# Second MoE: the transposes of an item's third and fourth tile put into branches on the item's count

## The chip, the cores and the metric

One core of one Trainium2 chip runs the kernel. The metric is the device time of one execution in microseconds (us), as the median of several runs. The profile is of one further execution of the same program on the chip.

## The reference, cut to what matters

Three layers follow one another: windowed attention, a gated feed-forward layer (called the first MoE here, though it has one expert), and a mixture of eight experts (the second MoE), which is the part that the change touches:

```python
x = _moe_ref(x=x, **moe_kwargs)                 # 2304 rows of 512
logits = x @ w_gate                             # 8 experts
expert_idx = np.argmax(logits, axis=1)
...
for e in range(8):
    mask = expert_idx == e
    xe = x[mask]
    h = np.maximum(xe @ w1[e], 0.0)             # 512 -> 1024
    ye = h @ w2[e]                              # 1024 -> 512
    out[mask] = gate_w[mask, None] * ye
```

How many rows an expert gets depends on the data and is known only while the kernel runs.

## The kernel before

The second MoE works through nine **items**. An item is a number of tiles of 128 rows of one expert: items 0 and 1 are the first and the second pair of tiles of expert 0, items 2 to 8 are four tiles each of experts 1 to 7. (Rows beyond 512 of one expert are done in a loop behind it, `L1200`, that is skipped when there are none.) Each item has eight steps f = 0 to 7, one for each 128 of the 1024 hidden columns. In a step TensorE does `first_mm` (rows by w1, 12 matmuls: four pieces of the depth by three products, since every float32 operand is split into a high and a low part), and `out_c` for the step before (hidden by w2, three matmuls of 512 columns for each tile of rows). ScalarE and VectorE make the ReLU and its two parts (`relu`), and split the weights of two steps ahead (`c_split`).

The order on each engine is as written out by hand in the loop over `steps2`; the compiler reorders nothing. All engines run their own list in order and wait for each other by semaphores.

**The count.** Only the rows that an expert has are worth computing. `load_count` (L1007) reads the count of an item's expert from SBUF into a register of TensorE. `cases` (L1029) then makes a tree of branches on TensorE alone, with one arm for each multiple of 64 rows from 256 to 512: `first_mm` runs over that many columns and `out_c` over that many tiles. For items 2 to 8 an arm is reached by two or three comparisons, in item 1 by one. The first two tiles are always done.

**The transposes.** The rows of the next item lie in SBUF with a row on each partition, and `first_mm` needs them transposed. `c_transpose(i, j, bk)` does tile j of item i: four TensorE transposes (L890) into one PSUM bank, ScalarE's copy of it (L892, the high part) and VectorE's subtraction (L893, the low part). Tiles 0 to 3 of item i + 1 are transposed at the ends of the steps f = 2, 3, 4 and 5 of item i, into banks 2 and 3 in turn. All four are done whatever the count.

So at the end of step f = 4 of item i, TensorE's list is: the arm of `cases`, `out_c` of tiles 0 and 1 (six matmuls, the last of them `bank<-who,hl`), the four transposes of tile 2, and then the comparisons of `cases` of step 5. In step f = 5 `load_count(i + 1)` stands ahead of the transposes of tile 3.

Of the kernel before, what the change touches and what calls it, by code (L numbers as in the profile page):

```python
# [26 lines left out]
P = 128  # L27
# [26 lines left out]
def attention_moe_moe_kernel(ctx, tc, qT, kT, vw, w1p, rms_g, wg2, wg2T, w2p, out):  # L54
    nc = tc.nc
# [14 lines left out]
    ident = const.tile([P, P], F32, name="ident")  # L70
# [53 lines left out]
    def xt_views(at, n):  # L124

        return [xt_t[:, a:a + 4 * n].rearrange("p (c t) -> p c t", c=4) for a in (at, at + 4 * n)]
# [160 lines left out]
    def beside(tasks, budget, fresh=True):  # L287

        for t in tasks if fresh else []:
            t.rest = 0.0  # L290
        while budget > 0:
            can = [t for t in tasks if not t.done and t.rest <= 0 and t.want != "bank"
                   and not (callable(t.want) and not t.want())]
            if not can:
                break
            cost = can[0].piece()
            budget -= cost
            for o in tasks:
                if o is not can[0]:
                    o.rest -= cost  # L300
        return budget

    def on_bank(tasks, bk):

        for t in tasks:
            if t.want == "bank" and not t.done:
                return t.piece(bk)
        return 0.0
# [395 lines left out]
    def out_b(u):  # L704
        k, i = units[u]
        last_mm(k, ("b", u), enumerate(out_banks(i)), u == starts[i], u == stops[i])
# [3 lines left out]
    def evac(u):  # L710
        k, i = units[u]
        n = steps[k][0]
        if u != stops[i]:
            return 0.0
        t0, nt, _ = subs[i]
        for j, bk in enumerate(out_banks(i)):
            x2 = x2_p.tile([P, DM], F32, name="x2")
            (nc.vector.tensor_copy if j % 2 else nc.scalar.copy)(x2, bk)
            x2_t.setdefault(n, []).append(x2)
            nc.sync.dma_start(x2dram[t0 + j * P:t0 + (j + 1) * P], x2)  # L720
        if i == blocks[n][2][-1]:
            put[0] = n
        return 0.6
# [119 lines left out]
    items = [(0, 0, 2), (0, 2, 2)] + [(e, 0, 4) for e in range(1, E)]  # L843
    steps2 = [(i, f) for i in range(len(items)) for f in range(NF2)]
    K0 = len(steps)
    ix_t, xg_t = {}, {}
# [11 lines left out]
    def c_split(k, hold=False, parts="ao"):  # L858
        if k < len(steps2):
            rest = w_split(K0 + k, ("c", k), wring[w_index(k) % NRING], 512, {"a": nc.vector, "o": nc.vector},  # L860
                           parts)
            if not hold:
                for _, r in rest:
                    r()
            if k >= NF2 and "o" in parts:
                later.append(w_index(k) + NRING)
            return rest
# [15 lines left out]
    def c_transpose(i, j, bk):  # L883
        if i >= len(items) or j >= items[i][2]:
            return
        if j == 0:
            xh_t["c", i], xl_t["c", i] = xt_views(i % 2 * 8 * 512, 512)
        xh, xl, ts = xh_t["c", i], xl_t["c", i], slice(j * P, (j + 1) * P)
        for c in range(4):
            nc.tensor.transpose(bk[:, c * P:(c + 1) * P], xg_t[i][:, j, c * P:(c + 1) * P], ident)  # L890
        b3 = bk.rearrange("p (c t) -> p c t", c=4)
        nc.scalar.copy(xh[:, :, ts], b3)  # L892
        nc.vector.tensor_tensor(out=xl[:, :, ts], in0=b3, in1=xh[:, :, ts].bitcast(F32), op=ALU.subtract)  # L893
# [38 lines left out]
    for u, (k, i) in enumerate(units):  # L932
# [7 lines left out]
        if len(blocks[n][2]) > 1:  # L940
            bk = bank[1]
        else:
            bk = bank[4] if n == len(blocks) - 1 else bank[5]
# [58 lines left out]
    count = {}  # L1002
# [18 lines left out]
    def cases(i, body, unit=P // 2):  # L1021

        e, t0, T = items[i]

        def between(lo, hi):
            if lo == hi:
                return body(lo * unit)
            mid = (lo + hi) // 2
            with tc.If(count[e] > t0 * P + mid * unit) as more:  # L1029
                between(mid + 1, hi)  # L1030
            with more.Else():
                between(lo, mid)

        if i == 0:
            body(T * P)
        elif T == 4:
            between(2 * P // unit, T * P // unit)
        else:
            unit = P
            between(1, T)  # L1040

    def first_mm(k, n):
        i, f = steps2[k]
        wh, wl = wh_t[K0 + k, "a"], wl_t[K0 + k, "a"]
        xh, xl, n = xh_t["c", i], xl_t["c", i], max(n, 2 * P)
        for c in range(4):
            w = slice(c * P, (c + 1) * P)
            split_mm(bank[k % 2][:, :n], wh[:, w], wl[:, w], xh[:, c, :n], xl[:, c, :n], c == 0, c == 3)

    def relu(k):  # L1050
        n = items[steps2[k][0]][2] * P
        if k == NL - 1:
            hh, hl = (xt_t[:, a:a + 512] for a in (16 * 512, 17 * 512))
        else:
            hh, hl = (h_p.tile([P, 512], F32R, name=x) for x in ("hh", "hl"))
        hh_t[K0 + k], hl_t[K0 + k] = hh, hl
        nc.scalar.activation(hh[:, :n], bank[k % 2][:, :n], AF.Relu, scale=1.0)  # L1057
        nc.vector.scalar_tensor_tensor(out=hl[:, :n], in0=bank[k % 2][:, :n], scalar=0.0, in1=hh[:, :n].bitcast(F32),  # L1058
                                       op0=ALU.max, op1=ALU.subtract)

    def out_c(k, n, j0=0):
        f = steps2[k][1]
        last_mm(K0 + k, K0 + k, [(j, bank[4 + j]) for j in range(j0, -(-n // P))], f == 0, f == NF2 - 1)
# [14 lines left out]
    def c_out(i, tiles=None):  # L1078
        ix = ix_t[i]
        for j in tiles or range(items[i][2]):  # L1080
            y = x2_p.tile([P, DM], F32, name="x2")
            gw = ix[:, j, 1:2].bitcast(F32)
            if j % 2:
                nc.vector.tensor_scalar_mul(y, bank[4 + j], gw)
            else:
                nc.scalar.activation(y, bank[4 + j], AF.Copy, scale=gw)  # L1086
            d = nc.gpsimd.indirect_dma_start(out=out[:, :], in_=y, in_offset=None,  # L1087
                                             out_offset=bass.IndirectOffsetOnAxis(ap=ix[:, j, 0:1], axis=0),
                                             bounds_check=NT - 1, oob_is_err=False)
            tc.declare_no_dep(d.ins, group="out", reason="a token has one expert: the rows differ")  # L1090
            tc.add_to_no_dep_group("out", d.ins)
# [44 lines left out]
    for k, (i, f) in enumerate(steps2):  # L1136
        if i == 0:
            for now in range(2):
                if now == (k > 1):
                    first_mm(k, 2 * P)  # L1140
                elif k > 0:
                    on_bank([end], bank[3])
                    beside([end], 99)
            if k == 0:
                out_b(len(units) - 1)
            else:
                out_c(k - 1, 2 * P)
        elif i == 1:
            if f < 2:
                if f == 0:  # L1150
                    out_c(k - 1, 2 * P)
                first_mm(k, 2 * P)
                if f == 1:
                    cases(i, lambda n: out_c(k - 1, n))
            else:
                cases(i, lambda n: (first_mm(k, n), out_c(k - 1, n)))
        elif f > 0:
            cases(i, lambda n: (first_mm(k, n), out_c(k - 1, n, 2)))
            if k < NL - 1:
                out_c(k - 1, 2 * P)  # L1160
        else:
            j0 = 0 if i == 2 else 1
            cases(i, lambda n: first_mm(k, n))
            out_c(k - 1, j0 * P)
            cases(i - 1, lambda n: out_c(k - 1, n, j0), P)
        relu(k)
        if k == 0:
            evac(len(units) - 1)
        if f == 0 and i > 0:
            c_split(k + 2, parts="a")  # L1170
            c_out(i - 1)
            c_split(k + 2, parts="o")
        else:
            c_split(k + 2)
        while i > 0 and later:
            c_load(later.pop(0))
        if i == 0:
            if f == NF2 - 1:
                end.finish(bank[3])
                load_count(1)  # L1180
                for j in range(2):
                    c_transpose(1, j, bank[2 + j % 2])
            continue
        if f == 5:
            load_count(i + 1)
        beside([over], 0.4)
        if i == len(items) - 1 and f == 3:

            nc.gpsimd.drain()
        if f in (2, 3, 4, 5):  # L1190
            c_transpose(i + 1, f - 2, bank[2 + f % 2])
        if f == 6:
            c_gather(i + 2)
# [6 lines left out]
    with tc.If(n_over > 0):  # L1200
        with tc.For_i(0, n_over, 1) as i:
            ex = nc.values_load(slot[0:1, bass.ds(i, 1)], engines=(ET.SP,), min_val=0, max_val=E - 1)
            row = nc.values_load(slot[0:1, bass.ds(i + NS, 1)], engines=(ET.SP,), min_val=0, max_val=E * NT - 2 * P)
            with tc.tile_pool(name="ovr", bufs=1) as o_p:
# [14 lines left out]
                for f in range(NF2):  # L1219
                    bk = bank[2 + f % 2][:, :2 * P]  # L1220
# [58 lines left out]
```

## Time and profile before

| | us |
|---|---|
| median of 3 runs | 831.22 (829.57 to 832.62) |
| the profiled execution, its own time | 828.35 |
| its span in the trace | 826.6 |

The span is what the trace covers, from the first to the last instruction; the profiled execution's time is 1.75 us longer, for what lies around it. In the views, PE is TensorE's matmuls, PEld its weight loads, DVE is VectorE, ACT ScalarE, POOL GpSimd, SP SyncE. A letter q behind an engine marks its sequencer: waits, branches, register work. A row such as `bank<-xt,wha` says what an instruction writes and reads. L60 is the helper that issues every matmul. Matmuls are pipelined, and the end of each is modelled by the profiler, so the time from one start to the next is the better measure of what one costs.

### The profile page before, as it was taken

To read this page: it belongs to the slowest core of one execution; us is meant where nothing else is said; L and a number is where in the kernel's file an instruction comes from. 1 tells how busy PE (TensorE), PEld (TensorE's weight loads), DVE (VectorE), ACT (ScalarE), POOL (GpSimd) and SP (SyncE) were. 2 spreads that over 40 slices of the span, in tenths; PEclk is the share of its full clock that TensorE was granted. 3 is DMA by queue.
4 is the path that set the end of the run, shared out by engine and by line. 5 is a ranking of instruction groups with operands and counts; after the bars stand their busy time and mean duration, and the time that the engine had idled before them with its cause. 6 is when DMAs were issued, how large, how long until landed. Compare 5 with 4: busy or idle time off the path is not lost. (4 is left out here: it accounts for less than half of the span.)

```text
span 826.6 us, 13258 instructions
## 1 busy us (share of the span) xinstructions
PE 806.6 (98%) x4777; PEld 746.5 (90%) x4777; DVE 566.7 (69%) x1210; ACT 431.1 (52%) x839; POOL 222.1 (27%) x194
## 2 busy tenths in 40 slices
PE   7999999999999999999999999999899999999997
PEld 7999989899999999999899999999788999888886
DVE  6898777777754766763389869846595765776454
ACT  5878877677633323322343333434564654765353
POOL 7989444334340000015000006031300220222021
PEclk9999999999999999999999999999999999999999
DMA  8999679889422101002110023861675763772010
GB/s 273 327 294 303 154 183 249 224 174 273 128 103 77 38 1 39 1 1 76 40 38 1 1 81 112 266 170 62 159 252 193 232 231 113 260 252 81 2 45 22
DMA packets 76179, 114.33 MB, mean 138 GB/s; under 512 B 28847, under 2 KB 45615, under 8 KB 75954
## 3 DMA queue, kind: packets, MB, share of 16 engines
q1 hardware_dynamic: 71506, 103.50, 42.5%
q0 software_dynamic: 4576, 9.47, 3.1%
q8 instruction: 69, 1.13, 0.6%
q14 instruction: 28, 0.23, 0.1%
HBM read 93.90 MB, written 31.10 MB: 151 GB/s over the span
## 5 line engine op out<-in xcount | busy, mean ns | idle before, releaser
L60 PE MATMUL bank<-xt,wha 128*128 128x384 f32 (+3 forms) x1728 | 417.9, 327 | 1.9 <-ACT xt L892 1.3
L60 PEld LDWEIGHTS bank<-xt,wha 128*128 128x128 f32 x1728 | 301.8, 188 | 10.9 <-ACT xt L892 1.5
L60 PE MATMUL bank<-xt,wla 128*128 128x384 f32 (+3 forms) x864 | 280.0, 324 | 0.3 <-DVE wla L576 0.3
L60 PEld LDWEIGHTS bank<-xt,wla 128*128 128x128 f32 x864 | 162.7, 188 | 1.0 <-DVE wla L576 0.6
L60 PE MATMUL bank<-who,hl 128*128 128x512 f32 x382 | 150.2, 393 | 1.0 <-DVE hl L1058 0.6
L60 PE MATMUL bank<-who,hh 128*128 128x512 f32 x382 | 150.3, 393 | 0.2 <-ACT x L1086 0.2
L60 PE MATMUL bank<-wlo,hh 128*128 128x512 f32 x382 | 149.4, 391 | 0.0
L685 ACT CAST hh<-t 128x384 fp32r<-128x384 f32 x72 | 37.0, 514 | 149.4 <-DVE t L684 149.4
L576 DVE TENSOR_TENSOR wla<-wraw,wha 128x512 fp32r<-128x512 f32 (+1 forms) x113 | 99.2, 878 | 15.9 <-ACT wha L574 15.2
L1058 DVE SCALAR_TENSOR_TENSOR hl<-bank,hh 128x512 fp32r<-128x512 f32 (+1 forms) x71 | 44.7, 629 | 70.9 <-ACT hh L1057 70.8
L684 DVE TENSOR_TENSOR t<-t,bank 128x384 f32<-128x384 f32 x72 | 39.7, 552 | 74.1 <-PE bank L60 67.9
L574 ACT CAST wha<-wraw 128x512 fp32r<-128x512 f32 (+1 forms) x113 | 87.0, 770 | 6.0 <-DVE wraw L426 5.8
L1087 POOL DMA_INDIRECT out_dram<-x,ix x32 | 34.8, 1086 | 204.1 <-ACT x L1086 196.6
L60 PEld LDWEIGHTS bank<-who,hl 128*128 128x128 f32 x382 | 71.8, 188 | 18.2 <-DVE hl L1058 1.4
L1057 ACT ACTIVATE hh<-bank 128x512 fp32r<-128x512 f32 (+1 forms) x71 | 39.0, 550 | 89.3 <-PE bank L60 89.3
L60 PEld LDWEIGHTS bank<-who,hh 128*128 128x128 f32 x382 | 72.0, 189 | 10.4 <-ACT x L1086 0.4
L60 PEld LDWEIGHTS bank<-wlo,hh 128*128 128x128 f32 x382 | 72.0, 189 | 10.2
L574 ACT CAST who<-wraw 128x512 fp32r<-128x512 f32 x111 | 68.7, 619 | 17.5 <-PE bank L60 17.5
L749 DVE SCALAR_TENSOR_TENSOR junk<-x,wg_bc 128x512 f32<-128x512 f32 x120 | 76.6, 685 | 0.0
L576 DVE TENSOR_TENSOR wlo<-wraw,who 128x512 fp32r<-128x512 f32 x99 | 68.2, 689 | 8.6 <-ACT who L574 3.4
L683 ACT ACTIVATE t<-bank 128x384 f32<-128x384 f32 x72 | 35.0, 486 | 65.7 <-PE bank L60 62.7
L797 POOL TENSOR_TENSOR tot<-tot,ohb 128x8 f32<-128x8 f32 x18 | 4.5, 251 | 237.6 <-DVE de L781 236.5
(154 smaller groups left out, 969.9 us busy)
## 6 DMA issues: line engine op xcount, KB each, us to landing
wraw<-in_w2p_dram SPq DMA_DIRECT2D x64, 512.0 KB, 4.6
st<-in_w1p_dram SPq DMA_DIRECT2D x24, 768.0 KB, 7.3
wraw<-in_vw_dram SPq DMA_DIRECT2D x16, 512.0 KB, 5.9
xs<-x2dram SPq DMA_DIRECT2D x8, 1024.0 KB, 12.8
qs<-in_qT_dram SPq DMA_DIRECT2D x16, 288.0 KB, 5.9
xdram<-wraw SPq DMA_DIRECT2D x32, 144.0 KB, 4.6
x2dram<-x SPq DMA_DIRECT2D x18, 256.0 KB, 2.0
kt<-in_kT_dram SPq DMA_DIRECT2D x15, 288.0 KB, 5.4
```

The source lines that it names most:

```text
L60: nc.tensor.matmul(o, l, r, start=start, stop=stop)
L574: nc.scalar.copy(wh, src[:, r])
L576: e.tensor_tensor(out=wl, in0=src[:, r], in1=wh.bitcast(F32), op=ALU.subtract)))
L683: nc.scalar.activation(t, g, AF.Silu, scale=1.0)
L684: nc.vector.tensor_tensor(out=t, in0=t, in1=v, op=ALU.mult)
L685: nc.scalar.copy(hh[:, :nt], t)
L749: nc.vector.scalar_tensor_tensor(out=junk, in0=x2, scalar=1.0, in1=wg_bc[:, e], op0=ALU.mult, op1=ALU.mult, accum_out=lg[:, j, e:e + 1])
L797: nc.gpsimd.tensor_tensor(out=tot, in0=tot, in1=ohb[:, j], op=ALU.add)
L1057: nc.scalar.activation(hh[:, :n], bank[k % 2][:, :n], AF.Relu, scale=1.0)
L1058: nc.vector.scalar_tensor_tensor(out=hl[:, :n], in0=bank[k % 2][:, :n], scalar=0.0, in1=hh[:, :n].bitcast(F32), op0=ALU.max, op1=ALU.subtract)
L1087: d = nc.gpsimd.indirect_dma_start(out=out[:, :], in_=y, in_offset=None, out_offset=bass.IndirectOffsetOnAxis(ap=ix[:, j, 0:1], axis=0), b ...
```

## The change

For the third and fourth tile of an item (j = 2 and 3) the four transposes stand in a branch of TensorE that is taken only if the count of the item's expert reaches into that tile. ScalarE's copy and VectorE's subtraction stay outside and run in any case. Since the count is now needed by step f = 4, it is loaded in step f = 2 and no longer in step f = 5. Items 2 to 8 have a third and a fourth tile, so there are 14 such branches.

```diff
@@ -886,8 +886,16 @@
         if j == 0:
             xh_t["c", i], xl_t["c", i] = xt_views(i % 2 * 8 * 512, 512)
         xh, xl, ts = xh_t["c", i], xl_t["c", i], slice(j * P, (j + 1) * P)
-        for c in range(4):
-            nc.tensor.transpose(bk[:, c * P:(c + 1) * P], xg_t[i][:, j, c * P:(c + 1) * P], ident)
+
+        def turn():
+            for c in range(4):
+                nc.tensor.transpose(bk[:, c * P:(c + 1) * P], xg_t[i][:, j, c * P:(c + 1) * P], ident)
+
+        if j < 2:
+            turn()
+        else:
+            with tc.If(count[items[i][0]] > j * P):
+                turn()
         b3 = bk.rearrange("p (c t) -> p c t", c=4)
         nc.scalar.copy(xh[:, :, ts], b3)
         nc.vector.tensor_tensor(out=xl[:, :, ts], in0=b3, in1=xh[:, :, ts].bitcast(F32), op=ALU.subtract)
@@ -1181,7 +1189,7 @@
                 for j in range(2):
                     c_transpose(1, j, bank[2 + j % 2])
             continue
-        if f == 5:
+        if f == 2:
             load_count(i + 1)
         beside([over], 0.4)
         if i == len(items) - 1 and f == 3:
```

## Rows read from the trace of the kernel before

**Rows 1.** The page, busy time: engine, busy us, share of the span, instructions.

```profile
PE 806.6 (98%) x4777; PEld 746.5 (90%) x4777; DVE 566.7 (69%) x1210; ACT 431.1 (52%) x839; POOL 222.1 (27%) x194
```

**Rows 2.** Busy time by stretch of the second MoE, with clock and DMA share.

```profile
core 0: us, PE busy (x) PEld busy (x) DVE busy (x) ACT busy (x) POOL busy (x), PEclk, DMA share, GB/s
585.00:600.00 15.00, 12.07 (x78) 10.06 (x77) 7.96 (x16) 7.39 (x15) 2.47 (x4) 1.00 0.68 196
...
655.00:700.00 45.00, 45.00 (x259) 40.91 (x258) 29.02 (x45) 25.16 (x45) 4.82 (x4) 1.00 0.54 180
...
735.00:745.00 10.00, 8.72 (x57) 7.55 (x57) 6.55 (x11) 5.62 (x11) 2.38 (x2) 1.00 0.90 312
745.00:815.00 70.00, 70.00 (x388) 62.30 (x387) 40.72 (x63) 35.02 (x62) 8.74 (x8) 1.00 0.10 36
```

**Rows 3.** Groups by form on PE: first_mm of items 2 to 8, in order.

```profile
L60 PE MATMUL bank<-xt,wha 128*128 128x320 f32 x64 | 14.7, 315 | 0.2 <-ACT wha L574 0.2
...
L60 PE MATMUL bank<-xt,wha 128*128 128x256 f32 x63 | 11.8, 284 | 0.0
...
L60 PE MATMUL bank<-xt,wha 128*128 128x384 f32 x56 | 14.6, 341 | 0.0
...
L60 PE MATMUL bank<-xt,wha 128*128 128x256 f32 x64 | 12.1, 286 | 0.0
...
L60 PE MATMUL bank<-xt,wha 128*128 128x256 f32 x64 | 12.0, 285 | 1.3 <-ACT xt L892 1.3
...
L60 PE MATMUL bank<-xt,wha 128*128 128x448 f32 x61 | 17.6, 368 | 0.0
...
L60 PE MATMUL bank<-xt,wha 128*128 128x256 f32 x54 | 9.9, 280 | 0.0
```

**Rows 4.** PE's timeline (start us, us), a step's end with and without transposes.

```profile
715.51 0.39 PE L60 MATMUL bank<-who,hl 128*128 128x512 f32 x1
715.75 0.60 PE L890 MATMUL bank<-ident,xr 128*128 128x128 f32 x4
716.10 0.48 PE L60 MATMUL bank<-xt,wha 128*128 128x256 f32 x2
716.42 0.28 PE L60 MATMUL bank<-xt,wla 128*128 128x256 f32 x1
...
666.38 0.40 PE L60 MATMUL bank<-xt,wha 128*128 128x256 f32 x2
666.63 0.28 PE L60 MATMUL bank<-xt,wla 128*128 128x256 f32 x1
```

**Rows 5.** L1029's branches, a step's three, and PE's timeline where that step begins.

```profile
L1029 PEldq COMPARE_BRANCH  x3: 208/208/208, 742.4 to 742.9; - x3
...
745.07 0.48 PE L60 MATMUL bank<-xt,wha 128*128 128x256 f32 x2
```

**Rows 6.** L1200, a skipped branch (min/median/max ns, first and last start); PE's last matmul.

```profile
L1200 PEldq COMPARE_BRANCH  x1: 342/342/342, 818.6 to 818.6; - x1
...
L1200 PEldq EVENT_SEMAPHORE  x1: 51/51/51, 820.9 to 820.9; - x1
...
820.49 0.40 PE L60 MATMUL bank<-who,hl 128*128 128x512 f32 x1
```

**Rows 7.** L1029's branches at the start of item 2, and PE's timeline there.

```profile
L1029 PEldq COMPARE_BRANCH  x3: 70/208/208, 612.3 to 612.8; - x3
...
612.27 0.49 PE L60 MATMUL bank<-who,hl 128*128 128x512 f32 x1
612.93 0.55 PE L60 MATMUL bank<-xt,wha 128*128 128x320 f32 x2 [0.16 <-ACT wha L574]
```

**Rows 8.** L1029's branches in all, and those of two steps of item 5.

```profile
L1029 PEldq COMPARE_BRANCH  x200: 70/208/3600, 593.6 to 814.9; - x100
...
L1029 PEldq COMPARE_BRANCH  x3: 208/208/697, 713.4 to 714.5; - x3
...
L1029 PEldq COMPARE_BRANCH  x3: 208/208/637, 716.7 to 717.6; - x3
```

**Rows 9.** L1029's longest branch, and PE's timeline behind it.

```profile
L1029 PEldq COMPARE_BRANCH  x3: 208/208/3600, 737.6 to 741.5; - x3
...
739.93 0.60 PE L890 MATMUL bank<-ident,sq 128*128 128x128 f32 x4
741.81 0.50 PE L60 MATMUL bank<-xt,wha 128*128 128x256 f32 x2 [1.28 <-ACT xt L892]
```

**Rows 10.** L1007's loading of a count in item 1, and PE's timeline there.

```profile
L1007 PEldq TENSOR_LOAD <-cnt x1: 329/329/329, 607.0 to 607.0; - x1
...
607.25 0.40 PE L60 MATMUL bank<-who,hl 128*128 128x512 f32 x1
607.67 0.65 PE L890 MATMUL bank<-ident,xr 128*128 128x128 f32 x4
```

## The prediction

> **What bounds the kernel now.** I read the page first: TensorE is busy 806.6 of 826.6 us, VectorE 69%, ScalarE 52% [rows 1]. Then the stretches of the second MoE: PE fills 45.00 of 45.00 us and 70.00 of 70.00, and what it misses lies at the start and in 735 to 745 [rows 2]. So a microsecond that TensorE saves or loses here moves the end by the same. [...]
>
> Next, what is skipped. The widths of first_mm tell each item's count within 64: 320, 256, 384, 256, 256, 448, 256 for items 2 to 8 [rows 3]. The third tile is needed above 256, so in items 2, 4 and 7; the fourth above 384, in item 7 alone. Of 14 branches four run their transposes and ten skip them.
>
> What remains is the branch itself. PE's timeline shows no branch, so I asked for the branches by their source line. Three comparisons start at 742.4 to 742.9, but the step that they choose begins on PE at 745.07 [rows 5]: TensorE's sequencer runs about 2.4 us ahead of its matmuls, and under that lead the branches of today cost nothing. The question is whether the new ones leave the lead alone.
>
> **What the change removes.** From the last who,hl matmul of a step to the next first_mm is 0.59 us (715.51 to 716.10), 0.35 of it the four transposes (715.75 to 716.10). Behind transposes the first pair of matmuls also goes slower: 716.10 to 716.42 against 666.38 to 666.63, 0.07 us [rows 4]. Ten skips would give 10 x (0.35 + 0.07) = 4.2 us, if nothing took their place.
>
> **What it adds in a skip.** The last transpose raises TensorE's semaphore, by which ScalarE's copy knows that the bank is filled. A path around it must raise it too. The kernel has one branch without an else that is skipped already, L1200: TensorE's comparison ends at 818.6 + 0.34 = 818.9, and then an EVENT_SEMAPHORE of that same line comes, but only at 820.9, when PE's last matmul, begun at 820.49, has ended at 820.89 [rows 6]. So a skipped branch makes up for the missed increment in the sequencer, and waits for every matmul issued before. The arms of L1029 escape that because each holds matmuls; an empty arm does not. I therefore expect each of the ten skips to **drain TensorE**, and with it the 2.4 us of lead goes.
>
> Queued behind that wait is all of TensorE: next in its list are the comparisons of the next step's cases, then the first weight load. They now pass in the open. With S the start of the last who,hl: the semaphore instruction comes at S + 0.41 to 0.45 (820.49 to 820.9, read to a tenth), takes 0.05 [rows 6], and a hand-over in the sequencer takes some 0.06, so the sequencer is free at S + 0.55.
>
> The price of open comparisons is shown at the start of item 2, where the lead is gone: comparisons of 208, 208 and 70 ns run from 612.3, and first_mm starts at 612.93, although the matmul ahead had started at 612.27 [rows 7]. That is 0.66 us for two of 208 and one of 70 ns, which fits 0.27 for each of the first kind and 0.13 for the second, hand-overs included. (The row blames ACT for the gap; the comparisons explain it.) I read 208 ns as a comparison that goes to its else arm, as all three do at width 256 [rows 5], and 70 ns as one that falls into its then arm.
>
> By widths [rows 3], a skip in an item costs, start of first_mm after against S + 0.59 before:
> - items 3 and 5 (width 256, three of 208): S + 0.55 + 0.81 = S + 1.36, so 0.77 us, three times: 2.31;
> - item 2 (320): S + 0.55 + 0.67 = S + 1.22, 0.63 us, twice: 1.26;
> - items 4 and 7 (384 and 448, one of 208 and one of 70): S + 0.95, 0.36 us, four times: 1.44;
> - item 1 (one of 208): S + 0.82, 0.23 us, once.
>
> Sum 5.24 us. The skips counted are those of the next item's tiles, done in the steps of the item named. The 0.07 us of a slow start stays, since first_mm behind an open branch starts slowly too (612.93). The skip's own comparison lies under the matmuls still queued, so nothing is added for it.
>
> [...]
>
> **Late comparisons.** Some take longer than 208 ns: 637 and 697 in the sets ahead of the two steps of item 5 that would follow a skip, up to 3600 in all [rows 8]. Today the lead hides them, save one: the 3600 ns one began at 737.9 and held PE from 739.93 + 0.35 to 741.81, about 1.5 us [rows 9]. In the open all of the excess counts. Added over the ten sets that would be exposed, it is 1.7 us in this execution, of which item 5's two sets are 0.49 + 0.43 [rows 8]. Bounds: nothing, if the wait gives time to have the instructions at hand, and 10 x 0.49 = 4.9 if every set were as late as the worst of item 5. I take 1.7, since it is the same code at the same places.
>
> **What it moves.** The loading of the count goes from f = 5 to f = 2, the same instructions, no DMA. In items 2 to 7 the lead hides it at both places. In item 1 there is little lead: it begins at 607.0 and the transposes start at 607.67, 0.42 us behind the matmul ahead where 0.24 is usual [rows 4, 10]. That 0.18 goes, and about 0.3 comes at f = 2, where PE waits for VectorE and the lead is just as small: 0.1 net, between 0 and 0.4.
>
> **What stays.** The four branches that run: a 70 ns comparison and a jump over the else path, under the lead: 0 us, up to 4 x 0.3 = 1.2 if it is short. ScalarE's copy and VectorE's subtraction run as before; PE waits on neither in the full stretches [rows 2]. GpSimd, SP and the DMA queues get nothing new.
>
> **Sum:** 5.2 + 1.7 + 0.1 = 7.0 us slower. The profiled execution of 828.35 would become 835.4. It stood 2.9 us below the median of 831.22, so against that median I forecast 838.2.
>
> **Rivals.**
> - *The skip does not drain* (faster). If the increment is made up without waiting for earlier matmuls, the lead survives and PE goes from who,hl to first_mm in 0.23 us, as where no transposes stand. Then all 4.2 us come back, less 0.1: 827.1. For it: PE is full and removed work counts whole [rows 2]. Against it: the two idle microseconds of L1200's semaphore [rows 6]. It decides if the semaphore instruction of a skip runs while PE still has matmuls queued. 0.13.
> - *The drain is cheap* (within 0.3%, that is 2.5 us, about what a measurement of this kernel can tell from no change). PE's ends are modelled; if the semaphore rises nearer to the next usual start, S + 0.23, each skip is 0.2 us cheaper, and with no late comparisons the sum falls to 5.2 - 2.0 = 3.2; with the one 1.5 us hold-up [rows 9] gone as well, 1.7 remain: 832.9. 0.07.
> - *Code comes late in the open* (slower still). Every comparison after a drain that has to wait as at 737.9 now costs 3.4 us over its 208 ns instead of 1.5 [rows 9]. If three of ten sets met that, 10 us come on top of 7: 848. For it: the long one fell where DMA was busy to 0.90 [rows 2]. Against it: one in 200 branches was so long, and the median is 208 [rows 8]. 0.08. [...]
> - *The branches skip nothing*: excluded by the widths, unless counts are read wrongly [rows 3].
>
> **How the numbers follow.** Drain with exposed comparisons: 0.72, with 834 (no late ones, early semaphore) to 845 (4.9 for late ones, 1.2 for the branches that run, 0.4 for the load, and some of the timed runs' own spread of 3 us). With the rival beyond it, slower by over 0.3% has 0.80; within has 0.07; faster 0.13. The range from 831.5 to 846 leaves out the faster case and most of the late-code one, and takes in the cheap drain.
>
> **What would show it.** Right: ten EVENT_SEMAPHOREs on TensorE's sequencer at the new branch's line, each just after a who,hl has ended; behind them gaps of 0.8 to 1.4 us from who,hl to first_mm, longest in items 3 and 5; 88 transposes of L890 in place of 128; PE's busy share down. Comparisons in f = 5 and f = 6 stand just ahead of their first_mm and no longer 2.4 us. Wrong: who,hl followed by first_mm in 0.23 us at a skip, or semaphore instructions that start while matmuls are still queued; late comparisons of a microsecond behind most skips would mean that the third rival holds.

## The result and the profile after

The change makes the kernel slower: median 840.33 us (836.48 to 846.56, 4 runs) against 830.39 (828.8 to 832.62), ratio 1.0117 with a 95% interval of 1.007 to 1.0165. Of the four runs two took 836.5 and 836.7 us at a mean granted clock of 0.998 and 0.999, and two took 844.0 and 846.6 us at 0.993 and 0.992. The profiled execution took 836.48 us, 8.13 more than that of the kernel before.

The page of the changed kernel, busy time:

```profile
PE 802.7 (96%) x4737; PEld 740.5 (89%) x4737; DVE 566.8 (68%) x1210; ACT 431.3 (52%) x839; POOL 222.7 (27%) x194
```

The forty transposes are gone (4737 matmuls for 4777, [rows 1]) and PE is busy 4 us less, in a longer span. So the time went into waiting. Next, the groups of the transposes, and the line of the new branch (min/median/max ns, first and last start):

```profile
L892 PE MATMUL bank<-ident,xr 128*128 128x128 f32 x48 | 7.2, 273 | 0.7 <-issue 0.7
L892 PE MATMUL bank<-ident,sq 128*128 128x128 f32 x40 | 5.9, 273 | 1.5 <-DMA sq<-xs 1.5
```

```profile
L897 PEldq COMPARE_BRANCH  x18: 70/205/208, 603.2 to 788.6; - x18
L897 PEldq EVENT_SEMAPHORE  x10: 51/51/51, 607.4 to 792.7; - x10
```

88 transposes are left of 128, and there are ten EVENT_SEMAPHOREs, one for each skip. (The 18 comparisons are 14 at the branch and four jumps behind the transposes that ran.)

One skip in item 3, from the timeline and from the sources of the new branch and of `cases`, which is now L1037:

```profile
665.82 0.40 PE L60 MATMUL bank<-who,hl 128*128 128x512 f32 x1
667.21 0.39 PE L60 MATMUL bank<-xt,wha 128*128 128x256 f32 x1 [0.99 <-ACT who L574]
...
L897 PEldq EVENT_SEMAPHORE  x1: 51/51/51, 666.3 to 666.3; - x1
...
L1037 PEldq COMPARE_BRANCH  x3: 208/208/208, 666.4 to 666.9; - x3
```

The last matmul ends at 666.22, the semaphore instruction comes at 666.3, then the three comparisons pass one after the other with PE idle, and first_mm starts 1.39 us behind the start of who,hl, where 0.59 was usual with the transposes in between [rows 4]. The view puts the idle time down to a wait for ACT; the comparisons that end just before the restart are the better reading. In the kernel before, comparisons stood 2.4 us ahead of their step [rows 5].

The same in items 5 and 4:

```profile
723.48 0.40 PE L60 MATMUL bank<-who,hl 128*128 128x512 f32 x1
...
L1037 PEldq COMPARE_BRANCH  x3: 208/208/421, 724.1 to 724.9; - x3
...
725.13 0.50 PE L60 MATMUL bank<-xt,wha 128*128 128x256 f32 x2 [1.26 <-ACT xt L900]
...
693.57 0.39 PE L60 MATMUL bank<-who,hl 128*128 128x512 f32 x1
694.54 0.61 PE L60 MATMUL bank<-xt,wha 128*128 128x384 f32 x2 [0.59 <-PEq L897]
```

Three comparisons with a late one take 1.65 us; two of 208 and 70 ns take 0.97. Here the view names the sequencer at L897 itself.

Two other places grew. In item 1 the count is now loaded where nothing covers it, and in items 3 and 6 a late comparison held PE. The load (L1015) and its step, then the late comparisons of items 3 and 6:

```profile
L1015 PEldq TENSOR_LOAD <-cnt x1: 860/860/860, 598.2 to 598.2; - x1
...
598.24 0.49 PE L60 MATMUL bank<-who,hl 128*128 128x512 f32 x1 [0.61 <-DVE hl L1066]
599.49 0.66 PE L892 MATMUL bank<-ident,xr 128*128 128x128 f32 x4 [0.75 <-issue]
...
L1037 PEldq COMPARE_BRANCH  x3: 208/208/3930, 655.3 to 659.6; - x3
...
657.63 0.60 PE L892 MATMUL bank<-ident,xr 128*128 128x128 f32 x4
659.90 0.39 PE L60 MATMUL bank<-xt,wha 128*128 128x256 f32 x1 [1.67 <-ACT xt L900]
...
L1037 PEldq COMPARE_BRANCH  x3: 208/208/3973, 744.4 to 748.8; - x3
...
746.76 0.60 PE L892 MATMUL bank<-ident,sq 128*128 128x128 f32 x4
749.02 0.50 PE L60 MATMUL bank<-xt,wha 128*128 128x256 f32 x2 [1.66 <-ACT xt L900]
```

**The account of the 8.1 us**, from the starts in PE's timeline. The ten distances from who,hl to first_mm sum to 12.86 us, where ten of 0.59 make 5.9: 6.96 more. The two late comparisons hold PE for 1.92 and 1.91 us beyond the 0.35 of the transposes, where the kernel before had one of 1.53 [rows 9]: 2.30 more, though neither stands behind a skip. The load costs 0.92 at f = 2 (598.24 to 599.49, where the kernel before had 599.50 to 599.83) and gives back 0.18 at f = 5: 0.74 more. The comparisons at the start of item 2, open before [rows 7], are covered now: 0.43 less. And the first transposes of item 1 started 1.24 us earlier in this execution (589.01 against 590.25), ahead of everything that was changed. That is 8.3, against 8.13 measured.

Behind the earlier start stands the clock. In the layer ahead of the second MoE the profile of the kernel before has a stretch at a granted clock of 0.50, and that of the change has none (first the kernel before, then the change; the clock stands behind the engines):

```profile
569.30:572.70 3.40, 3.40 (x14) 3.11 (x14) 2.76 (x14) 1.11 (x3) 0.60 (x3) 0.50 0.00 0
569.30:572.70 3.40, 3.40 (x26) 2.95 (x26) 2.51 (x15) 1.11 (x3) 0.60 (x3) 1.00 0.00 0
```

The same work around it, from 24 matmuls of 8 columns that start at 566.22 on, took 7.05 us before and 5.49 after; what else differs ahead of item 1 comes to 0.3 the other way. So 8.13 understates what lies behind the start: there the terms make 9.6, where the medians differ by 9.9. Of it 7.3 are the skips, the load and the covered comparisons; that the 2.3 of the late comparisons belong to the change isn't shown (see the third rival below).

### The profile page after: what moved, and what is told of

It is laid out like the page before. It is cut to its first block, busy times and chain, and to the rows that moved or that the text cites. A ratio compares the mean times of both kernels' runs of the same rounds, so it can differ in the third digit from the quotient of the medians.

```text
span 834.7 us, 13206 instructions
## 1 busy us (share of the span) xinstructions
PE 802.7 (96%) x4737; PEld 740.5 (89%) x4737; DVE 566.8 (68%) x1210; ACT 431.3 (52%) x839; POOL 222.7 (27%) x194
## 3 DMA queue, kind: packets, MB, share of 16 engines
q8 instruction: 69, 1.13, 0.6%
## 5 line engine op out<-in xcount | busy, mean ns | idle before, releaser
L202 POOL TENSOR_SCALAR qz<-qs 64x576 f32<-64x576 f32 x29 | 65.3, 2250 | 10.1 <-DMA qs<-in_qT_dram 8.4
```

What stands on the lines that cost most here:

```text
L202: (nc.gpsimd if u else nc.vector).tensor_scalar(out=q_t[u][r, c, r], in0=qs[r, c], scalar1=0.125, scalar2=None, op0=ALU.mult)
```

## The experiments

Two theories. **Drain**: a skip waits for every matmul before it and so loses the sequencer's lead; what costs is that wait and the comparisons that then stand open. **Late code**: 14 more branches make more branches late, wherever they are. (A ratio below is an estimate over all runs of both kernels and need not be the quotient of the two medians beside it; times with "slower" go by its interval.)

### Same branch, else arm with one small matmul

```diff
-            with tc.If(count[items[i][0]] > j * P):
+            with tc.If(count[items[i][0]] > j * P) as more:
                 turn()
+            with more.Else():
+                mm(bk[:, :E], ones_b, lt_b[:, :E], True, True)
```

> The branch is kept, and its else arm gets one small matmul (8 columns, into the same bank; nobody uses what it writes). Drain theory: the missed increment now rides on that matmul as in the arms of cases, no EVENT_SEMAPHORE with a wait stands in the skip, the lead survives; each of ten skips saves 0.35 + 0.07 us less about 0.03 for the small matmul, 3.9 us in all, and the moved count load costs 0.7 in item 1: about 3 us faster than before (827). Late-code theory (the cost is the fetch of code behind 14 more branches): the branches are all still there, so it stays 6 to 10 us slower than before.

Measured: 828.72 us against 831.2, ratio 0.9967 (0.9947 to 0.9988). Its branch line has the same 18 comparisons and jumps and no EVENT_SEMAPHORE at all. The branch's source, and a skip of item 2 in PE's timeline:

```profile
L897 PEldq COMPARE_BRANCH  x18: 70/208/208, 600.7 to 776.4; - x18
...
627.80 0.40 PE L60 MATMUL bank<-who,hl 128*128 128x512 f32 x1
628.04 0.18 PE L60 MATMUL bank<-lt_b,ones_b 128*128 128x8 bf16 x1
628.08 0.54 PE L60 MATMUL bank<-xt,wha 128*128 128x320 f32 x2
```

From who,hl to first_mm it is 0.28 us, where the change had 1.36 and 1.46 in item 2. All branches are still there, and the loss is gone: this decides for the drain. It is also faster than both kernels.

### Both arms with all transposes

```diff
-            with tc.If(count[items[i][0]] > j * P):
+            with tc.If(count[items[i][0]] > j * P) as more:
                 turn()
+            with more.Else():
+                turn()
```

> Both arms of the branch hold the four transposes, so nothing is skipped and 14 branches are added. Drain theory: no drain, the comparisons lie under the lead; only the moved load remains: 0 to 1.5 us slower than before. Late-code theory: 14 more branches and more code to jump over cost as much as in the change: 6 to 10 us slower.

Measured: 833.16 us against 831.2, ratio 1.0028 (1.0006 to 1.0051), that is 0.5 to 4.2 us slower. Fourteen branches without a drain, and the moved load, cost some 2 us and not 8. What there is above the expected 1.5 this run doesn't settle.

### The skip ahead of six matmuls

```diff
             cases(i, lambda n: (first_mm(k, n), out_c(k - 1, n, 2)))
+            if f in (4, 5):
+                c_transpose(i + 1, f - 2, bank[2 + f % 2], 0)
             if k < NL - 1:
                 out_c(k - 1, 2 * P)
```

(Here part 0 of `c_transpose` is TensorE's alone; the other two engines' parts come where they were. Item 1 is as in the change.)

> In items 2 to 7 the branch with the transposes of tiles 2 and 3 stands ahead of the six matmuls of out_c for tiles 0 and 1, so that these, and no comparisons, come next behind a skip; ScalarE's and VectorE's parts stay where they were. Drain theory: the ten semaphore waits are still there (nine of them moved), but a skip now costs S + 0.55 + 0.06 against S + 0.59 before, and the comparisons pass under 1.4 us of out_c: 0 to 2.5 us slower than before, 6 to 9 us faster than the change. Late-code theory: as many branches, so 6 to 10 us slower than before.

Measured: 832.14 us against 831.2, ratio 1.0015 (0.999 to 1.0039). The branch's source, a skip of item 4 in the timeline, and the two comparisons and a jump of its next step, which run while out_c does:

```profile
L899 PEldq EVENT_SEMAPHORE  x10: 51/51/51, 609.4 to 786.5; - x10
...
689.51 0.40 PE L60 MATMUL bank<-who,hl 128*128 128x512 f32 x1
690.06 0.47 PE L60 MATMUL bank<-who,hh 128*128 128x512 f32 x1
690.37 0.39 PE L60 MATMUL bank<-wlo,hh 128*128 128x512 f32 x1
...
L1041 PEldq COMPARE_BRANCH  x3: 70/176/208, 690.1 to 691.3; - x3
```

The ten waits are all there, and a skip costs 0.55 us from who,hl to the next matmul, where 0.23 is usual: 0.32 more, about what the transposes took. So the wait by itself only eats the gain. The loss of the change, about 1% more than this, is what stood open behind the wait.

### The drain without the saving

```diff
-        if j < 2:
-            turn()
-        else:
+        turn()
+        if j >= 2:
             with tc.If(count[items[i][0]] > j * P):
-                turn()
+                mm(bank[5 - bank.index(bk)][:, :E], ones_b, lt_b[:, :E], True, True)
```

> All transposes are done as before, and behind those of tiles 2 and 3 stands a branch on the count around one small matmul (8 columns into the other of the two banks, used by nobody), with no else. So the ten drains are there and nothing is saved. Drain theory: the sequencer is free when the last transpose has ended, S + 0.83 + 0.15 = S + 0.98, and the comparisons follow: 0.43 us a skip more than in the change, 4.3 us in all, so 12 to 14 us slower than before. If a skip's cost were in the transposes left out and not in the wait: about as before.

Measured: 846.19 us against 829.01, ratio 1.0178 (1.0127 to 1.0228): 10.5 to 18.9 us slower, the interval around the expected 12 to 14. A skip of item 4 in the timeline:

```profile
699.07 0.39 PE L60 MATMUL bank<-who,hl 128*128 128x512 f32 x1
699.30 0.60 PE L892 MATMUL bank<-ident,sq 128*128 128x128 f32 x4
700.49 0.61 PE L60 MATMUL bank<-xt,wha 128*128 128x384 f32 x2 [0.58 <-ACT who L574]
```

With all transposes done it is 1.42 us to first_mm, 0.45 more than the change's 0.97 in the same step (0.43 expected). The ten distances sum to 17.0 us, 4.2 more than the change's 12.86 (4.3 expected). The cost goes with the wait, whatever is skipped.

### The change again, and the load alone

The changed kernel itself ran once more:

> The changed kernel itself, for a narrower interval and a second profile. Drain theory: the ten skips cost 7.0 us as in the first profile (1.08 to 1.65 us from who,hl to first_mm in place of 0.59), the load 0.7, the rest is late comparisons that differ from run to run: 7 to 10 us slower than before.

Measured: 838.02 us against 829.01, ratio 1.0102 (1.0051 to 1.0153). Its ten distances are 0.98 to 1.60 us and sum to 12.8; in the first profile they were 0.97 to 1.65 and summed to 12.86.

```diff
-        if f == 5:
+        if f == 2:
             load_count(i + 1)
```

> The kernel before with the count loaded in step f = 2, and nothing else. In the profile of the change the load stood open in item 1: 0.9 us more at f = 2, 0.19 less at f = 5. So 0.7 us slower than before, which this many runs can just not tell from nothing. If the load were what costs in the change: 6 to 10 us slower.

Measured: 830.29 us against 829.01, ratio 1.0012 (0.9979 to 1.0044). The load can't be told from nothing, and isn't the 1%.

### The load one step later, with the small matmul

```diff
-        if f == 2:
+        if f == 3:
             load_count(i + 1)
```

> The branch with the small matmul in its else arm, and the count loaded in step f = 3, where PE waits for no other engine in item 1. If the load at f = 2 costs 0.7 us, this is 0.5 to 0.9 us faster than with the load at f = 2, that is 3.2 to 3.6 faster than before; if the load is hidden anyway, about 2.7 faster, as that one was.

Measured: 828.2 us against 829.01, ratio 0.9973 (0.9942 to 1.0004). In its trace item 1's load takes 0.31 us and no microsecond stands open there, but the time can't be told from that of the load at f = 2. Inconclusive for the load.

### What the removed transposes are worth

```diff
-            with tc.If(count[items[i][0]] > j * P):
+            if (i, j) in ((2, 2), (4, 2), (7, 2), (7, 3)):
                 turn()
```

> No branch at all: the ten groups of transposes that the counts of these inputs skip are left out when the kernel is written (right for these inputs alone), the load stays at f = 2. It measures what the removed transposes are worth. Both theories: 10 x 0.42 = 4.2 us less, 0.7 more for the load, about 3.5 us faster than before. If removed transposes are hidden anyway: no difference from before.

Measured: 829.86 us against 831.2, ratio 0.9983 (0.9961 to 1.0005). That is 1.4 us, not 3.5: a miss for both theories. In its profile two late comparisons hold PE in item 6, from the sources and the timeline:

```profile
L1037 PEldq COMPARE_BRANCH  x3: 208/208/3050, 729.3 to 732.7; - x3
...
730.37 0.40 PE L60 MATMUL bank<-who,hl 128*128 128x512 f32 x1
732.95 0.50 PE L60 MATMUL bank<-xt,wha 128*128 128x256 f32 x2 [2.19 <-issue]
...
L1037 PEldq COMPARE_BRANCH  x2: 208/1972/3735, 747.9 to 748.1; - x2
...
750.16 0.40 PE L60 MATMUL bank<-who,hl 128*128 128x512 f32 x1
751.93 0.39 PE L60 MATMUL bank<-xt,wha 128*128 128x256 f32 x1 [1.38 <-ACT who L574]
```

2.35 and 1.54 us over the usual 0.23, where the kernel before lost 1.5 to one [rows 9]; a third, in item 5, holds PE for 0.6. Behind the first the clock fell to 0.50 for 3.4 us as well (733.80 to 737.20; last section), which costs an estimated 1.6, as the same 3.4 us at 569.3 did in the kernel before. That is some 4.6 us more than before, enough to explain the 3.7 by which this execution (828.56 us, the kernel before 828.35) missed the forecast. Whether it does so in the timed ones, and whether fewer matmuls between branches are why, wasn't tried.

## Why the prediction was right

**What bounds the kernel**: right. PE was full, and what it lost moved the end. The sum has no term for the clock, and inside the second MoE none was missing in either profile of the change (in the first the clock was 1.00 in every stretch from 585 to 815 us). Whether that holds for the two timed runs at 0.992 and 0.993 isn't known, since they left no trace.

**What is skipped**: right, ten of 14; 88 transposes and ten semaphore instructions.

**The wait of a skip**: right, and it was the step that decided the sign. L1200's one row [rows 6] foretold all ten rows at L897; the else arm with a matmul shows, with no such row, that it is the empty arm that makes them.

**The open comparisons**: right in kind and nearly in size. At three comparisons without a late one 1.39 us against 1.36 foretold, at two 0.97 against 0.95. (The longest were in item 5, as foretold, but item 2's 1.46 is above item 3's 1.39.) With the late ones the ten skips cost 6.96 us, and 5.24 + 1.7 = 6.9 was foretold. That they agree so closely is luck. The 1.7 counts a set that follows no skip: the 697 ns at 713.4 [rows 8] belong to the step that begins at 716.10 [rows 4], f = 4, behind the transposes of tile 1. The set behind item 5's second skip, ahead of f = 6, was this one of the kernel before:

```profile
L1029 PEldq COMPARE_BRANCH  x3: 208/208/208, 720.2 to 720.7; - x3
```

Without the 0.49 of the wrong set the ten sets of the kernel before have 1.2 us over 208 ns, and those of the change have 1.2 too (seven comparisons of 325 to 421 ns). The other 0.5 are 0.02 to 0.14 us in each distance, which the sum did not have.

**The moved load**: mis-sized. "0.1 net, between 0 and 0.4" was 0.7 in the trace, because the load itself took 0.86 us there and not the 0.33 of [rows 10]. At f = 2 of item 1 the wait for VectorE (0.61 us idle ahead of 598.24) had taken the lead away, as foretold, so all of that stood open.

**The third rival** did not come true where it was put: behind the ten skips no comparison took more than 421 ns, and 424 in the second profile. The two of 3.9 us stand ahead of steps that follow no skip. They outran a lead that was still there, as the one in the kernel before did, and gave 2.3 us to the account. That they come from the change isn't shown: the kernel with the load alone, which has none of the new branches, has a comparison of 3.2 us ahead of the same step of item 3, which holds PE for 1.1, and in the second profile of the change item 3 has no such hold.

```profile
L1029 PEldq COMPARE_BRANCH  x2: 208/1681/3154, 652.5 to 655.7; - x2
...
654.78 0.60 PE L890 MATMUL bank<-ident,xr 128*128 128x128 f32 x4
656.22 0.50 PE L60 MATMUL bank<-xt,wha 128*128 128x256 f32 x2 [0.84 <-ACT xt L892]
```

**The first rival**, a skip that doesn't drain, is what the kernel with the small matmul does, and its price was about right: 4.1 us less than the kernel before was foretold for it; with the matmul and the load as they are, 3 were expected and 2.5 came.

**The median**: 838.2 was foretold, a ratio of 1.0084 to the median known then; 1.0117 and 1.0102 were measured.

## What to carry to other kernels

Ask of every arm of a branch on one engine whether it holds an instruction of that engine. Here the 14 branches and the moved load cost some 2 us with transposes in both arms, and 9.9 with nothing in place of ten groups of them. The ten empty arms left ten EVENT_SEMAPHOREs; the one shown for item 3 came at 666.3, just behind the end of the last matmul at 666.22, and the comparisons that followed stood open: 0.97 to 1.65 us from who,hl to first_mm, where 0.59 was usual. Whether an empty arm does the same in another kernel, its trace has to show: look for EVENT_SEMAPHOREs at the branch's line. Two ways out were measured: a trivial instruction in the empty arm (0.3% faster than before here), and the branch put where plain work and not more branches comes next (level with before here).

## What was not expected

**A long comparison in item 6, in every profile.** Each of the ten profiles has a branch of 2.9 to 4.4 us among the steps of item 6, where the kernel before has its 3600 ns [rows 9] and the DMA share is 0.90 [rows 2]. The lead of 2.4 us doesn't cover it, and 1.1 to 2.4 us stand open.

The traces show what goes with such a branch. Of two DMA queues named "instruction" one, q8, moves 16 KB at a time (69 packets, 1.13 MB in the kernel before). In the second MoE TensorE has 98 branches of over 0.6 us in the ten traces, and 95 of them end 1.2 to 1.6 us after a transfer of that queue has ended; of the 1735 branches under 0.25 us 5% do. Two such transfers, each in a window of 0.1 us around its start: from 656.9 in the change (item 3, the branch ends at 659.25) and from 739.1 in the kernel before (item 6, the branch ends at 741.49). The numbers are packets, MB, and the share of 16 engines' time in that window, so that they took 0.97 and 1.01 us.

```profile
q8 instruction: 1, 0.02, 60.7%
q8 instruction: 1, 0.02, 63.4%
```

That a long branch waits for its code is the author's reading of times that go together; no run moved the code, so the cause is not shown. Why a transfer starts up to 2.0 us after its branch did, and why item 6 has one in every run, stays open.

**The clock behind some of these holds.** In the kernel with both arms PE stood idle for 1.96 us ahead of 736.28, and a microsecond after it went on the granted clock fell to the lower level for 3.4 us. Its stretches, with the clock behind the engines, and the timeline:

```profile
737.20:740.70 3.50, 3.50 (x13) 2.89 (x12) 1.29 (x2) 1.11 (x2) 0.76 (x1) 0.51 0.60 216
740.70:745.00 4.30, 4.30 (x32) 3.95 (x31) 2.75 (x5) 3.04 (x6) 0.00 (x0) 1.00 0.39 125
...
736.28 0.50 PE L60 MATMUL bank<-xt,wha 128*128 128x256 f32 x2 [1.96 <-issue]
...
738.64 0.63 PE L60 MATMUL bank<-wlo,hh 128*128 128x512 f32 x1
739.07 0.63 PE L60 MATMUL bank<-who,hl 128*128 128x512 f32 x1
```

At 0.51 the matmuls of 512 columns start 0.43 us apart and not 0.23. That makes the hold dearer than its own length. The clock fell as well in the kernel with the static skip, behind 2.19 us, in that with the load at f = 3, behind 1.93, and twice in that with the drain alone, behind 2.21 and 1.95. But it did not fall behind 1.84 us (the load alone), 2.08 (the skip ahead of six matmuls) and 2.26 (the drain alone, a third time), nor behind the idle time at 588 to 590 in the kernel before (clock 1.00, [rows 2]). And the fall at 569.3 in the kernel before has no idle time ahead of it: PE had just run the 24 matmuls of 8 columns, which the change ran too and kept its clock. So a hold of 1.8 to 2.3 us was followed by the lower level in some cases and not in others, and what decides it isn't shown.

**The load of a count** takes from 0.30 to 1.04 us for the same instruction, and 0.79 to 1.02 us wherever it stood at f = 2 of item 1. What sets the difference isn't shown.
